# New lengths in the layout's own clock, twelve more attention units on VectorE, and a new table of urgencies

## The chip, the cores and the metric

One core of one Trainium2 chip runs the whole program. The metric is the device time of one execution in microseconds. "Before" is the median of three executions; one further execution was recorded by the hardware profiler, and all instruction durations below come from that one.

## The reference

Two kinds of layer alternate twice over one sequence of 2048 rows of 512 numbers: attention with 32 heads of 16 and a single shared key and value head, then a gated mixer.

```python
def _A_ref(x, wq, wk, wv, wo):            # H = 32, Dh = 16
    q = (x @ wq).reshape(B, S, H, Dh) ...  # one k and one v for all heads
    scores = einsum('bhqd,bkd->bhqk', q, k) * Dh ** (-0.5)
    p = softmax(scores, axis=-1)
    o = einsum('bhqk,bkd->bhqd', p, v)
    return o.reshape(B, S, H * Dh) @ wo

def _B_ref(x, w_in, w_sp, b_sp, w_out):    # F = 1792, Fh = 896
    z = gelu(einsum('bsd,df->bsf', x, w_in))
    z1, z2 = z[..., :Fh], layernorm(z[..., Fh:])
    g = einsum('ts,bsf->btf', w_sp, z2) + b_sp
    return einsum('bsf,fd->bsd', z1 * g, w_out)

x = x + A(layernorm(x)); x = x + B(layernorm(x))   # and both once more
```

The scores are 32 x 2048 x 2048 numbers in each of the two attention layers, and every one of them needs an exponential.

## The kernel before

**Units and blocks.** Attention is cut into 32 groups for each layer. A group is one set of query rows and heads whose output is 128x512, and it meets 16 key tiles. One group against one key tile is a *unit*: 512 queries and heads in each of four row strips, so four *blocks* of 128x512 scores. A score block is a matmul of 32 contracted rows (L990), and up to four of them, in different row strips of TensorE, run side by side.

**Two ways to the exponential.** Most units go to ScalarE: `push_slot` puts three or two blocks into one of two fixed groups of PSUM banks (banks 0 to 2, banks 3 and 4, in turn), and one ScalarE instruction (L1016) turns them into `P_ring`, a ring of 20 blocks. Then one step of four matmuls (L1035), side by side in four column strips, adds the unit to the group's sum in bank 6. The other units go to VectorE (`block_dve`): each block gets a side bank (5 or 7), and VectorE turns it into 16-bit integers whose bits are read as bf16, an approximate power of two (L1134). When the unit's four blocks are there, three additions inside SBUF (L1147, L1149, L1151) make four shifted copies, and five steps of four matmuls (L1167) add the five, each with its own weight, to the group's sum. A VectorE unit so takes five steps on TensorE where a ScalarE unit takes one. The tiles of these units live in a ring of six in `big`, of which one unit uses five.

How many of a group's 16 key tiles go to VectorE is a digit of `ON_DVE`, one string for each layer, for groups 4 to 31. The first groups have fixed shares of their own (`ATT`).

**Everything else runs between the blocks.** While attention runs, the finished row tiles go on: the output projection (`wo_tiles`), layernorm (`ln_tiles`), the mixer's first product (`b_front`, L690 with `w_in_r`), and parts of the big product with `w_sp` (`mix_stage`, L690 with `z2n`), whose partial sums VectorE adds (L1498) and which go to DRAM and come back. After the last group of layer 1 only the rest of the mixer is left (`mix_late`, L684).

**Who sets the order.** Nothing is ordered at run time. `_Graph.schedule` walks through all operations with a clock of its own, engine by engine, from lengths written into the code (`dur`, and `lat` until a reader may start), and at each free engine picks the ready operation with the smallest priority. `URGENCY` adds a number between -3 and 3 to the priority of named parts (`unit.1.63 pe` is the matmuls of VectorE units of layer 1 when 63 groups have been opened). The chosen order is emitted as one fixed stream for each engine with semaphore waits; the chip then runs these streams. Lengths in the code therefore never change a duration on the chip, they change the order, and with it who waits for whom. TensorE charges `SWITCH` for a change of tiling (full array, 32-row strips, 32-column strips). If TensorE has been busy for less than 55% of the last 3.4 us on this clock, `filler` puts in matmuls with no effect on the result (L716 on a free bank, L724 adding zeros).

The lines that the diff touches in the old kernel:

```python
def dve(fn, us, r, w, prio=5):
    return op("dve", fn, us, r=r, w=w, prio=prio)
...
main["last"] = op("act", act_e, 0.065 + n * 0.4267, r=[tk], ...)
...
us += SWITCH if o.mode != last_mode else 0.0
...
ON_DVE = [[0] * 4 + [int(c) for c in s] for s in (
    "4344343435423243434344233232",
    "4344433444333433434433244221")]
```

Of the kernel before, what the change touches and what calls it, by code (L numbers as in the profile page):

```python
# [38 lines left out]
SWITCH = 0.105  # L39
PE_LAT = 0.20  # L40
SEM_LAT = 0.06
# [4 lines left out]
URGENCY = {  # L46
# [26 lines left out]
}  # L73
# [10 lines left out]
AHEAD_US = 1.0  # L84
AHEAD_EPS = 0.05
PAIRS = False
PAIR_AHEAD = 0.12
# [57 lines left out]
class _Graph:  # L145
# [70 lines left out]
    def schedule(self):  # L216
# [15 lines left out]
        free = {e: True for e in ENGS}  # L232
        last_mode = 0
        open_rows = frozenset()
        bank_free = [True] * 8
# [12 lines left out]
        def push(t, what, x):  # L248
            nonlocal cnt
            cnt += 1  # L250
            heapq.heappush(ev, (t, cnt, what, x))
# [145 lines left out]
        while True:  # L397
            moved = True
            while moved:
                moved = False  # L400
                for e in ENGS:
                    if free[e]:
# [18 lines left out]
                        if e == "pe":  # L421
                            us += SWITCH if o.mode != last_mode else 0.0
                            past.append((now + us, o.work))
                            last_mode = o.mode
                            if o.opens is not None:
                                pv_open = o.opens
                            if beside(o):
                                us = BESIDE
                                open_rows = open_rows | o.rows
                            else:  # L430
                                open_rows = o.rows
                        push(now + us, 0, e)
                        for x in (o,) if o.mate is None else (o, o.mate):
# [118 lines left out]
def bass_interleave_layers__grouped_kv_mqa__mixer_gmlp__prompt_kernel(  # L552
# [127 lines left out]
    def dve(fn, us, r, w, prio=5):  # L680
        return op("dve", fn, us, r=r, w=w, prio=prio)

# [187 lines left out]
    def ln_tiles(t0, n, xT, keys, per_tile, prio=5, by_dma=False):  # L870
# [3 lines left out]
        for t in ts:  # L874
            i = t % CT
            dve(lambda e, i=i, t=t: e.bn_stats(st1[:, i, :], X[:, t, :]), 0.66, [("X", t)], [("st1", i)], prio)  # L876
            if not by_pool:
                dve(lambda e, i=i: e.bn_aggr(mv1[:, i, :], st1[:, i:i + 1, :]), 0.18, [("st1", i)], [("mv1", i)], prio)
# [114 lines left out]
    def push_slot(n):  # L993
# [21 lines left out]
        def act_e(e):  # L1015
            return e.activation(P_ring[:, s0:s0 + n, :], bank32(b0, n).rearrange("p (k q) -> p k q", k=n), ACTF.Exp,  # L1016
                                scale=E_SCALE)
        main["last"] = op("act", act_e, 0.065 + n * 0.4267, r=[tk], w=[("P", s0 + k) for k in range(n)], prio=3)
        for k, (u, j) in enumerate(blocks):
# [95 lines left out]
    def block_dve(x, j, slot_op):  # L1115
# [14 lines left out]
        if slot_op is not None:  # L1130
# [4 lines left out]
            ph16[:, tiles[0], j * QC:(j + 1) * QC], bank32(tk.bank), PH_BIAS, 0.0, op0=ALU.add, op1=ALU.max),  # L1135
            0.66, [tk], BIG(tiles[0]) if k == 0 else [("phj", tiles[0], k)], P_R)
        if PAIRS:
# [5 lines left out]
        if k == 3:  # L1143
            spread["todo"].pop(0)
            base = BIG(tiles[0]) + [("phj", tiles[0], i) for i in range(1, 4)]
            r0, r2, r4 = tiles[0], tiles[2], tiles[4]
            dve(lambda e: e.tensor_scalar(ph16[:, r2, :], ph16[:, r0, :], float(PH_A[2]), None, op0=ALU.add), 0.63, base,  # L1147
                BIG(r2), P_PH)
            dve(lambda e: e.tensor_scalar(two_rows(tiles[1], tiles[3]), two_rows(r0, r2), float(PH_A[1]), None,  # L1149
                                          op0=ALU.add), 1.16, base + BIG(r2), BIG(tiles[1]) + BIG(tiles[3]), P_PH)  # L1150
            dve(lambda e: e.tensor_scalar(ph16[:, r4, :], ph16[:, r0, :], float(PH_A[4]), None, op0=ALU.add), 0.63, base,  # L1151
                BIG(r4), P_PH)
# [23 lines left out]
    def finish_group(gi):  # L1176
# [20 lines left out]
        if RECP and t0 < DT_O:  # L1197
            op("pool", lambda e: e.tensor_tensor(rden[:, par, :, :], src()[:, :, :, DH],  # L1198
                                                 mone[:, 0:1, None].to_broadcast([P, CT, 4]), ALU.pow),
               0.4 + 0.19 * 16, r=[tk, "mone"], w=[("rden", par)], prio=pr)  # L1200
        else:
# [354 lines left out]
    def sums_lead(n, chain):  # L1556
# [61 lines left out]
    ON_DVE = [[0] * 4 + [int(c) for c in s] for s in (  # L1618
        "4344343435423243434344233232",
        "4344433444333433434433244221")]  # L1620

# [62 lines left out]
```

## Time and profile before

| what | value |
|---|---|
| median of three executions | 1662.25 us (1659.72 to 1663.79) |
| the profiled execution, its own time | 1657.53 us |
| its span in the profile | 1655.7 us |
| granted TensorE clock | 0.999 |
| TensorE matmul busy | 1574.8 us (95%) |
| ScalarE busy | 1557.9 us (94%) |
| VectorE busy | 1454.4 us (88%) |
| GpSimd busy | 371.5 us (22%) |
| 1313 exponentials, L1016 | 1487.3 us busy |

Busy time is the union of an engine's instruction records. On VectorE and ScalarE a record outlasts the moment at which the next instruction starts, so a full engine is better counted by the steps from start to start. The busy time of TensorE also holds the fillers and the waiting inside a pipelined matmul.

### The profile page before, as it was taken

The numbers are of one execution on the slowest core, as the hardware profiler recorded it, in microseconds if no ns is written. First come the engines' busy times: TensorE is split into PE (matmuls) and PEld (weight loads), VectorE is DVE, ScalarE is ACT, GpSimd is POOL, SyncE is SP. The second block draws the span as 40 slices with busy tenths as digits, with TensorE's granted clock in tenths as the row PEclk, the third lists the DMA queues.
The fourth block names the chain that finished last, engine by engine and source line by source line (L and its number), as shares of the span: only waits on it lengthen the run. The fifth ranks groups of instructions, "written<-read, shape, count | busy, mean of one in ns | idle before, by whom it ended". The sixth has DMA issues, their size and how long they took to land.

```text
span 1655.7 us, 45720 instructions
## 1 busy us (share of the span) xinstructions
PE 1574.8 (95%) x20407; PEld 529.0 (32%) x20421; DVE 1454.4 (88%) x2248; ACT 1557.9 (94%) x1362; POOL 371.5 (22%) x481
## 2 busy tenths in 40 slices
PE   8899999999999999999999999999899999989999
PEld 3222223232332232334533222233233323323344
DVE  8999989998899898877869999899989999798677
ACT  7999999999999999999299999999999999999970
POOL 3131221213221114000531321211422112220012
PEclk9999999999999999999999999999999999999999
DMA  8000010101321240555511000100033102305665
GB/s 199 17 18 8 9 26 5 21 8 40 84 56 40 62 93 5 132 150 148 157 48 24 17 8 14 21 12 16 12 87 88 38 22 77 54 30 151 173 162 151
DMA packets 173270, 102.75 MB, mean 62 GB/s; under 512 B 135056, under 2 KB 145680, under 8 KB 173072
## 3 DMA queue, kind: packets, MB, share of 16 engines
q1 hardware_dynamic: 173072, 99.81, 23.9%
q8 instruction: 160, 2.62, 0.7%
q14 instruction: 38, 0.31, 0.1%
HBM read 36.34 MB, written 31.46 MB: 41 GB/s over the span
## 4 chain that ended last, share of the span: by engine, by line
ACT 78%; PE 19%; DVE 2%; issue 0%; DMA 0%; SPq 0%; POOL 0%; DVEq 0%
ACT P_ring L1016 76%; PE ps_all L690 7%; PE ps_all L990 4%; PE ps_all L684 4%; PE ps_all L1167 2%; PE ps_all L1035 2%; ACT z2n L1398 1%; DVE big L1134 0%; DMA X<-in_A_x_dram 0%; DVE st L1441 0%; ACT L1016 0%; ACT L1398 0%; PE ps_all L898 0%; PE ps_all L724 0%; PE ps_all L1573 0%
## 5 line engine op out<-in xcount | busy, mean ns | idle before, releaser
L1016 ACT ACTIVATE P_ring<-ps_all 128x1024 bf16<-128x1024 f32 (+1 forms) x1313 | 1487.3, 1352 | 13.1 <-PE ps_all L990 12.0
L990 PE MATMUL ps_all<-qT,kT_rep 32*128 32x512 bf16 x4096 | 593.0, 385 | 67.2 <-ACT P_ring L1016 59.2
L1134 DVE TENSOR_SCALAR big<-ps_all 128x512 int16<-128x512 f32 x816 | 540.2, 685 | 86.0 <-PE ps_all L990 78.8
L1198 POOL TENSOR_TENSOR rden<-o_rows,small 128x16 f32<-128x16 bf16 x56 | 177.6, 3172 | 742.6 <-DMA o_rows<-oT 742.6
L990 PEld LDWEIGHTS ps_all<-qT,kT_rep 32*128 32x128 bf16 x4096 | 148.9, 91 | 601.5 <-ACT P_ring L1016 507.5
L1167 PE MATMUL ps_all<-big,V_ph 128*32 128x512 bf16 x4080 | 337.7, 383 | 2.1 <-DVE big L1149 0.7
L1035 PE MATMUL ps_all<-P_ring,V_ph 128*32 128x512 bf16 x3280 | 310.7, 386 | 1.3 <-DVE oT L1238 0.6
L1149 DVE TENSOR_SCALAR big<-big 128x4096 int16<-128x4096 int16 x204 | 249.1, 1221 | 0.5
L1147 DVE TENSOR_SCALAR big<-big 128x2048 int16<-128x2048 int16 x204 | 140.6, 689 | 3.3 <-PE ps_all L1167 0.8
L1151 DVE TENSOR_SCALAR big<-big 128x2048 int16<-128x2048 int16 x204 | 138.9, 693 | 2.5 <-PE ps_all L1167 2.2
L1167 PEld LDWEIGHTS ps_all<-big,V_ph 128*32 128x32 bf16 x4080 | 92.8, 95 | 128.9 <-issue 60.7
L1035 PEld LDWEIGHTS ps_all<-P_ring,V_ph 128*32 128x32 bf16 x3280 | 81.1, 94 | 142.6 <-issue 116.9
L724 PE MATMUL ps_all<-ones,zeros 128*32 128x512 bf16 x1200 | 101.3, 386 | 0.0
L690 PE MATMUL ps_all<-xnTA,z2n 128*32 128x512 bf16 x1344 | 94.3, 381 | 0.1
L820 POOL TENSOR_TENSOR small<-st 128x4 f32<-128x4 f32 (+5 forms) x50 | 18.8, 392 | 325.4 <-DVE st L876 267.2
L1270 DVE TENSOR_TENSOR X<-ps_all,X 128x512 bf16<-128x512 f32 x64 | 43.9, 686 | 25.5 <-PE ps_all L690 15.7
L690 PE MATMUL ps_all<-w_in_r,xo 128*32 128x448 bf16 x960 | 60.5, 355 | 0.3 <-DVE big L1134 0.2
L1212 POOL TENSOR_TENSOR o_norm<-o_rows,rden 128x128 bf16<-128x128 bf16 x112 | 57.4, 533 | 4.3
L690 PE MATMUL ps_all<-xo,w_in_r 128*32 128x512 bf16 (+2 forms) x1120 | 55.7, 327 | 0.3 <-DVE z1c L1388 0.3
L1498 DVE TENSOR_TENSOR big<-ps_all,big 128x512 f32<-128x512 f32 x56 | 38.3, 686 | 19.2 <-PE ps_all L690 18.9
L1363 DVE CAST z2n<-ps_all 128x448 bf16<-128x448 f32 x60 | 37.2, 620 | 18.5 <-PE ps_all L690 18.1
L1547 POOL TENSOR_TENSOR z1c<-big,z1c 128x512 bf16<-128x512 f32 (+1 forms) x47 | 45.1, 979 | 34.1 <-DVE big L1542 33.7
(113 smaller groups left out, 1081.7 us busy)
## 6 DMA issues: line engine op xcount, KB each, us to landing
gp_scratch<-big SPq DMA_DIRECT2D x112, 256.0 KB, 2.2
big<-gp_scratch SPq DMA_DIRECT2D x98, 256.0 KB, 3.0
big<-gp_scratch SPq DMA_DIRECT2D x28, 128.0 KB, 2.8
out_dram<-X SPq DMA_DIRECT2D x16, 128.0 KB, 2.4
w_in_r<-in_B_w_in_dram SPq DMA_DIRECT2D x1, 1792.0 KB, 8.3
X<-in_A_x_dram SPq DMA_DIRECT2D x3, 512.0 KB, 6.6
bsp<-in_B_b_sp_dram SPq DMA_DIRECT2D x8, 128.0 KB, 3.9
w_out_r<-in_B_w_out_dram SPq DMA_DIRECT2D x1, 896.0 KB, 5.5
```

The source lines that it names most:

```text
L684: return e.matmul(out, w, mv, start=start, stop=stop)
L690: ins = e.matmul(out[32 * j:32 * j + 32, :], w[:, 32 * j:32 * j + 32], mv, tile_position=(0, 32 * j), start=start, stop=stop)
L724: ins = e.matmul(bank32(PVB)[32 * j:32 * j + 32, :], zeros[:, 0:32], mv, tile_position=(0, 32 * j), start=False, stop=False)
L990: return e.matmul(out, kT_rep[32 * j:32 * j + 32, a, u[1] * P:(u[1] + 1) * P], qT[32 * j:32 * j + 32, q, :], tile_position=(32 * j, 0), st ...
L1016: return e.activation(P_ring[:, s0:s0 + n, :], bank32(b0, n).rearrange("p (k q) -> p k q", k=n), ACTF.Exp, scale=E_SCALE)
L1035: ins = e.matmul(bank32(PVB)[32 * j:32 * j + 32, :], V_ph[:, NPH, kt, :], P_ring[:, s, :], tile_position=(0, 32 * j), start=first, stop=last)
L1134: o = dve(lambda e: e.tensor_scalar(ph16[:, tiles[0], j * QC:(j + 1) * QC], bank32(tk.bank), PH_BIAS, 0.0, op0=ALU.add, op1=ALU.max), 0.66 ...
L1147: dve(lambda e: e.tensor_scalar(ph16[:, r2, :], ph16[:, r0, :], float(PH_A[2]), None, op0=ALU.add), 0.63, base, BIG(r2), P_PH)
L1149: dve(lambda e: e.tensor_scalar(two_rows(tiles[1], tiles[3]), two_rows(r0, r2), float(PH_A[1]), None, op0=ALU.add), 1.16, base + BIG(r2), ...
L1151: dve(lambda e: e.tensor_scalar(ph16[:, r4, :], ph16[:, r0, :], float(PH_A[4]), None, op0=ALU.add), 0.63, base, BIG(r4), P_PH)
L1167: ins = e.matmul(bank32(PVB)[32 * j:32 * j + 32, :], V_ph[:, a, kt, :], big[:, tiles[a], j * QC:(j + 1) * QC], tile_position=(0, 32 * j), ...
L1198: op("pool", lambda e: e.tensor_tensor(rden[:, par, :, :], src()[:, :, :, DH], mone[:, 0:1, None].to_broadcast([P, CT, 4]), ALU.pow), 0.4 ...
```

## The change

The `dve` helper now plans an instruction 85 ns shorter and lets its reader start 75 ns after that; several VectorE lengths are raised by some 25 or 60 ns ahead of this; the exponential is planned 12 ns shorter with 230 ns until its reader; the change of tiling is charged only as far as TensorE was not idle just before; TensorE's own delay to a reader goes from 0.20 to 0.15 us; one GpSimd length is lowered. Twelve units net go from ScalarE to VectorE: five in layer 0 (groups 8, 11, 16, 17, 22 and 23 get one more, group 27 one less) and seven in layer 1 (groups 5, 8, 14, 23 and 24 one more, group 26 two more). The table of urgencies is replaced. `SWIDLE` is defined and not used.

```diff
-PE_LAT = 0.20
+PE_LAT = 0.15
 URGENCY = {
-    "/b_front.0.0.4 pe": 1.5, "/b_front.0.0.4/ln_tiles.0.0.4": -3, "/b_front.0.12.3 pe": 0.5,
...
+    "/b_front.0.0.4 pe": 0.5, "/b_front.0.0.4/ln_tiles.0.0.4": -1.5, "/b_front.0.12.3 pe": -1,
...
+SWIDLE = 1.0
...
+        pe_end = 0.0
...
-                            us += SWITCH if o.mode != last_mode else 0.0
+                            us += max(0.0, SWITCH - (now - pe_end)) if o.mode != last_mode else 0.0
...
+                            pe_end = now + us
...
     def dve(fn, us, r, w, prio=5):
-        return op("dve", fn, us, r=r, w=w, prio=prio)
+        return op("dve", fn, max(0.06, us - 0.085), r=r, w=w, prio=prio, lat=0.075)
...
-        main["last"] = op("act", act_e, 0.065 + n * 0.4267, r=[tk], w=[("P", s0 + k) for k in range(n)], prio=3)
+        main["last"] = op("act", act_e, 0.053 + n * 0.4267, r=[tk], w=[("P", s0 + k) for k in range(n)], prio=3, lat=0.23)
...
             ph16[:, tiles[0], j * QC:(j + 1) * QC], bank32(tk.bank), PH_BIAS, 0.0, op0=ALU.add, op1=ALU.max),
-            0.66, [tk], BIG(tiles[0]) if k == 0 else [("phj", tiles[0], k)], P_R)
+            0.685, [tk], BIG(tiles[0]) if k == 0 else [("phj", tiles[0], k)], P_R)
...
-               0.4 + 0.19 * 16, r=[tk, "mone"], w=[("rden", par)], prio=pr)
+               2.98, r=[tk, "mone"], w=[("rden", par)], prio=pr, lat=0.17)
...
     ON_DVE = [[0] * 4 + [int(c) for c in s] for s in (
-        "4344343435423243434344233232",
-        "4344433444333433434433244221")]
+        "4344443535424343435444223232",
+        "4444533444433433434543444221")]
```

More of the change, by code (lines that the diff above doesn't have):

```diff
@@ L875, in ln_tiles @@
             i = t % CT
-            dve(lambda e, i=i, t=t: e.bn_stats(st1[:, i, :], X[:, t, :]), 0.66, [("X", t)], [("st1", i)], prio)
+            dve(lambda e, i=i, t=t: e.bn_stats(st1[:, i, :], X[:, t, :]), 0.685, [("X", t)], [("st1", i)], prio)
             if not by_pool:
@@ L1146, in block_dve @@
             r0, r2, r4 = tiles[0], tiles[2], tiles[4]
-            dve(lambda e: e.tensor_scalar(ph16[:, r2, :], ph16[:, r0, :], float(PH_A[2]), None, op0=ALU.add), 0.63, base,
+            dve(lambda e: e.tensor_scalar(ph16[:, r2, :], ph16[:, r0, :], float(PH_A[2]), None, op0=ALU.add), 0.69, base,
                 BIG(r2), P_PH)
             dve(lambda e: e.tensor_scalar(two_rows(tiles[1], tiles[3]), two_rows(r0, r2), float(PH_A[1]), None,
-                                          op0=ALU.add), 1.16, base + BIG(r2), BIG(tiles[1]) + BIG(tiles[3]), P_PH)
-            dve(lambda e: e.tensor_scalar(ph16[:, r4, :], ph16[:, r0, :], float(PH_A[4]), None, op0=ALU.add), 0.63, base,
+                                          op0=ALU.add), 1.22, base + BIG(r2), BIG(tiles[1]) + BIG(tiles[3]), P_PH)
+            dve(lambda e: e.tensor_scalar(ph16[:, r4, :], ph16[:, r0, :], float(PH_A[4]), None, op0=ALU.add), 0.69, base,
                 BIG(r4), P_PH)
```

56 rows, old and new, of the table URGENCY are left out of this document.

## The prediction

> **What bounds the kernel now.** I read the page's busy shares and its chain of waits first, then the groups kept apart by shape.
>
> ```profile
> span 1655.7 us, 45720 instructions
> ...
> PE 1574.8 (95%) x20407; PEld 529.0 (32%) x20421; DVE 1454.4 (88%) x2248; ACT 1557.9 (94%) x1362; POOL 371.5 (22%) x481
> ...
> ACT 78%; PE 19%; DVE 2%; issue 0%; DMA 0%; SPq 0%; POOL 0%; DVEq 0%
> ```
>
> ```profile
> L1016 ACT ACTIVATE P_ring<-ps_all 128x1536 bf16<-128x1536 f32 x655 | 1023.1, 1562 | 2.7 <-PE ps_all L990 1.7
> L1016 ACT ACTIVATE P_ring<-ps_all 128x1024 bf16<-128x1024 f32 x657 | 750.9, 1143 | 10.4 <-PE ps_all L990 10.3
> ...
> L1134 DVE TENSOR_SCALAR big<-ps_all 128x512 int16<-128x512 f32 x816 | 540.2, 685 | 86.0 <-PE ps_all L990 78.8
> ...
> L1149 DVE TENSOR_SCALAR big<-big 128x4096 int16<-128x4096 int16 x204 | 249.1, 1221 | 0.5
> ```
>
> Three engines look nearly full, but the chain of waits lies on ScalarE for 78% of the span, and its exponentials were kept waiting 13.1 us (2.7 and 10.4). VectorE's idle time stands ahead of L1134, where it waits for scores. The windows of busy time by stage, and VectorE's timeline:
>
> ```profile
> 898.20:1040.60 142.40, 134.08 (x1602) 39.70 (x1597) 135.42 (x196) 142.36 (x127) 34.17 (x24) 1.00 0.06 13
> 1040.60:1186.10 145.50, 135.29 (x1835) 44.10 (x1834) 134.44 (x205) 145.12 (x125) 35.76 (x48) 1.00 0.07 14
> ...
> 1513.50:1588.20 74.70, 74.11 (x1025) 24.22 (x1025) 46.59 (x76) 74.66 (x68) 1.92 (x7) 1.00 0.65 174
> 1588.20:1655.70 67.50, 63.32 (x464) 29.53 (x462) 55.62 (x99) 17.04 (x14) 17.79 (x16) 1.00 0.52 148
> ```
>
> ```profile
> 410.15 0.68 DVE L1270 TENSOR_TENSOR X<-ps_all,X 128x512 bf16<-128x512 f32 x1
> 410.74 0.68 DVE L1134 TENSOR_SCALAR big<-ps_all 128x512 int16<-128x512 f32 x1
> 411.34 0.68 DVE L1240 CAST oT<-ps_all 128x512 bf16<-128x512 f32 x1
> ```
>
> After span, the columns are TensorE, its weight loads, VectorE, ScalarE and GpSimd. The first two rows are groups 1 to 14 of layer 1: ScalarE is full (142.36 of 142.40). Just after the last group (fourth row) it has little to do, and TensorE is busy 63.32 of 67.50. The timeline shows why 685 ns is not what a VectorE instruction costs: the next starts 0.60 us later, 85 ns before the record ends. Counted so, by records less 85 ns, VectorE's work is 1386 us, 84% of the span. Exponentials likewise start 1.330 us apart behind one of three blocks and 0.903 behind one of two (medians of the starts), not 1.562 and 1.143. Counted so, ScalarE lost 20.6 us between exponentials (8.7 and 9.3 of it in the two layers' dense stretches, 77 to 671 us and 898 to 1513 us). It is the bound; VectorE has room.
>
> **ScalarE.** The changed kernel's order holds 646 exponentials of three blocks and 647 of two, where there were 655, 657 and one of a single block: 9 x 1.330 + 10 x 0.903 + 0.48 (0.903 less the 0.427 of one block) = 21.5 us less, nearly all on the path. One unit is 21.5 / 12 = 1.79 us.
>
> A rule of the Trainium skill (ScalarE: Activation LUTs, What ACT_TABLE_LOAD costs) prices an ACTIVATE at 186 ns plus 0.833 ns an element, with back-to-back ones overlapping by 93 ns; as an estimate from that page a step would be 1.372 or 0.946 us and the saving 22.3 us. The measured starts decide.
>
> **VectorE.** Twelve units add 48 of L1134 at 0.60 and twelve each of L1147, L1149 and L1151 at 0.60, 1.13 and 0.60 (records less 85 ns): 4.73 us a unit, 56.8 in all, 1386 to 1443 us. Over the whole span that fits. By stage it does not everywhere. I summed these costs over each stretch between the evacuations of groups (L1238, L1240), in the old order and the new, and set against them the length that ScalarE alone would allow (the measured one less 1.79 us for each unit taken away):
>
> | groups | before, VectorE of length | after, VectorE of ScalarE's length |
> |---|---|---|
> | layer 0, 4 to 14 | 221.3 of 248.0 (89%) | 231.0 of 244.4 (95%) |
> | layer 0, 15 to 26 | 248.3 of 290.5 (85%) | 261.0 of 283.4 (92%) |
> | layer 1, 1 to 14 | 259.9 of 287.9 (90%) | 275.3 of 282.5 (97%) |
> | layer 1, 15 to 23 | 179.7 of 202.7 (89%) | 186.2 of 200.9 (93%) |
> | layer 1, 24 to 28 | 105.6 of 124.7 (85%) | 113.8 of 119.3 (95%) |
>
> What counts is the share that VectorE can hold. The best that the trace shows is 95.1% over 60 us (from 64 us on) and 93.5% over 120 us, both while ScalarE set the pace, so neither is a ceiling; 100% would be one. At a share s each row takes the larger of its two times, and the excess over ScalarE's length sums to 0 at 98%, 4.3 at 96% (275.3 / 0.96 = 286.8), 7.8 at 95%, 13.5 at 94%, 20.5 at 93% and 24 at 92.5%. I take 95.5%, 6 us: just over the nearest row, since a VectorE that is late has its next work waiting.
>
> **TensorE.** A step of four side by side takes 0.217 us and a change of tiling 0.105:
>
> ```profile
> 402.19 0.39 PE L990 MATMUL ps_all<-qT,kT_rep 32*128 32x512 bf16 x3
> 402.51 0.62 PE L690 MATMUL ps_all<-z2n 128*32 128x512 bf16 x8
> 403.06 0.39 PE L990 MATMUL ps_all<-qT,kT_rep 32*128 32x512 bf16 x2
> ```
>
> Three scores and a change take 0.32 us, two steps and a change 0.55. The twelve units add 60 steps of L1167 and remove 12 of L1035, +10.4 us; fillers go from 325 to 307, -3.9. With the changes of tiling the orders sum to 1493 and 1501 us. In the attention stretches that is +2.6 us in layer 0 and -2.3 in layer 1, hidden behind ScalarE: TensorE between one exponential's scores and the next averages 1.064 us before and 1.076 after, against exponentials of 1.09.
>
> **The tail is not hidden.** Behind the last L1035 the new order puts 24 more steps of the mixer's second stage (5.2 us), 8 of `w_in` columns of 448 (1.5), 4 of width 384 (0.65) and two fillers less (-0.4); with changes of tiling 64.1 us become 70.6. TensorE's idle time there is 4.2 us (67.50 less 63.32), so the cost is between 2.3 and some 8 us, the upper end if the last tile's chain (output projection, layernorm, normalization), now queued behind 11 us of other matmuls, opens new gaps. I take 6: the old gaps are waits of that chain and stay. Between the layers TensorE, last on the path there, gets 41.1 to 42.7 us: +1, between 0 and 2. The other lengths only reorder: new GpSimd and delay constants change no count, and the DMA queue gets the same transfers; I price them at nothing, covered by ScalarE's backlog, or at the first rival's excess where that is gone.
>
> **Sum.** -21.5 + 6 + 1 + 6 = -8.5, say -9 us. The profiled execution took 1657.5 us (span 1655.7 and 1.8 around it) and would become 1648.5. The median, 1662.25, lies 4.7 above that execution; on it the forecast is 1653.
>
> **Rivals.**
> *VectorE becomes the bound (slower).* Place: groups 1 to 14 of layer 1, at 97% even without a stall, then groups 4 to 14 of layer 0. Mechanism: L1134 needs a score block in one of two side banks, the matmuls of a unit wait on TensorE's fixed queue for the additions, and the scores for ScalarE stand behind them. For it: the 78.8 us that L1134 waited for scores, so some idle time may be inherent. Against: much of that wait was pacing by ScalarE. At 92.5% the excess is 24 us and the sum +10: 1672. It decides at 94%, where the excess eats the 14.5.
> *The new order also removes stalls.* The new lengths match the measured steps (0.60; 1.333 and 0.906 against 1.330 and 0.903), the old ones were too long on VectorE by 0.06. If VectorE holds 97% or more (1 us) and 5 of the 20.6 lost us go: -18.5, 1644.
> *TensorE takes part.* Pairs of intervals in which TensorE's work exceeds the exponentials' rise from 375 to 444, their excess from 115 to 122 us. If all 7 reach the path: -1.5, 1661.
> *VectorE's additions collide with GpSimd.* The power at L1198 runs 178 us, 11% of the span. Were an addition that meets one held for half its 3.17 us, the 36 new ones would lose 36 x 0.11 x 1.6 = 6 us: -2.5, 1660. The trace speaks against it: L1149 waited 0.5 us in all over 204 and is no longer beside L1198 (1218 ns) than away from it (1221).
> The Trainium skill (SBUF — State Buffer, Who interferes with whom) states that rule: VectorE in a two-port mode and GpSimd share a port pair, and whichever comes second blocks fully. By it this rival would stand; the rows show VectorE not held.
> That the move does not happen is excluded by the count of exponentials.
>
> **How the numbers follow.** A measurement tells 0.3%, 5 us, from no change. Forecast 0.50 (0.44 of it beyond 5 us, 0.06 within), VectorE-bound 0.20, fewer stalls 0.13, TensorE 0.14 (0.03 faster, 0.09 same, 0.02 slower), port 0.03 (0.02 same, 0.01 slower). Faster 0.60, same 0.17, slower 0.23. The forecast's own range is 1646 to 1658 (share 94.5 to 98%, tail 2.3 to 8). For 8 in 10 it reaches into both neighbours: 1642 to 1668.
>
> **What would show it.** Right: 1293 exponentials, some 1466 us busy; idle time ahead of L1016 up from 13 to 15 to 25 us, mostly in layer 1's first 14 groups; VectorE near 95% there by steps; last exponential ending near 1573 us instead of 1587.5, and some 74 us behind it. Wrong: those 14 groups longer than 287.9 us (first rival), less idle time ahead of L1016 (second), or 68 us behind the last exponential, as before (the tail's 6).

## The result and the profile after

| | before | after |
|---|---|---|
| median of six executions | 1662.47 us (1658.42 to 1663.79) | 1653.18 us (1650.59 to 1654.32) |
| profiled execution, its own time | 1657.53 us | 1654.32 us |
| its span | 1655.7 us | 1652.5 us |

The ratio is 0.9945, with a 95% interval of 0.9931 to 0.9959: 9.3 us less, outside the 0.3% that a measurement tells from no change.

Not all of the 9.3 us belongs to the change. In many executions TensorE's granted clock falls to half for a few microseconds, at places that differ from run to run. Executions with a mean clock of 1.000 took 1656.1 to 1656.9 us before (measured beside the experiments) and 1650.59 and 1650.63 us after, so some 6 us are the change's; the rest is that the runs of before behind the median held more of these dips. Below, "undisturbed" means the length of a stage in a run that had no dip there; such lengths repeat to 0.1 to 0.4 us.

The page of the changed kernel, the lines that answer to those of before:

```profile
span 1652.5 us, 45935 instructions
...
PE 1590.0 (96%) x20490; PEld 538.2 (33%) x20490; DVE 1487.8 (90%) x2332; ACT 1544.7 (93%) x1342; POOL 372.3 (23%) x481
...
ACT 48%; PE 38%; DVE 12%; issue 1%; DMA 1%; POOL 0%; DVEq 0%; SPq 0%
...
L1025 ACT ACTIVATE P_ring<-ps_all 128x1024 bf16<-128x1024 f32 (+1 forms) x1293 | 1474.2, 1305 | 23.3 <-PE ps_all L999 19.9
```

The chain of waits, 78% on ScalarE before, is now 48% ScalarE, 38% TensorE and 12% VectorE. The exponentials (L1025, before L1016) are 20 fewer and waited 23.3 us for scores and buffers where they had waited 13.1. VectorE's groups (L1143 and L1158, before L1134 and L1149):

```profile
L1143 DVE TENSOR_SCALAR big<-ps_all 128x512 int16<-128x512 f32 x864 | 563.0, 681 | 44.8 <-PE ps_all L999 42.5
L1158 DVE TENSOR_SCALAR big<-big 128x4096 int16<-128x4096 int16 x216 | 263.2, 1218 | 0.7 <-PE ps_all L1176 0.2
```

VectorE now waits 44.8 us ahead of its score blocks, not 86.0: it took in 48 blocks more and nearly halved its idle time there. The additions still start without a wait (0.7 us over 216) and last as long as before (1218 against 1221 ns).

By stage, as in the prediction's table (a stage ends where a group's sum is taken out of bank 6). "Fewer exponentials" is 1.08 us, the 21.5 / 20 of the forecast, for each exponential that the stage lost or got; the last column is what the difference holds beyond that.

| stage | before | after | difference | forecast | exponentials | rest |
|---|---|---|---|---|---|---|
| layer 0, to group 3 | 112.6 | 107.7 | -4.9 | 0 | -3.2 | -1.7 |
| layer 0, 4 to 14 | 248.0 | 246.2 | -1.8 | -3.6 | 0 | -1.8 |
| layer 0, 15 to 26 | 290.5 | 287.2 | -3.3 | -7.2 | -8.6 | +5.3 |
| layer 0, 27 to 31 | 122.3 | 127.7 | +5.4 | +1.8 | +3.2 | +2.2 |
| between the layers | 124.8 | 119.6 | -5.2 | +1 | -2.2 | -3.0 |
| layer 1, 1 to 14 | 287.9 | 286.7 | -1.2 | +0.4 | -1.1 | -0.1 |
| layer 1, 15 to 23 | 202.7 | 205.4 | +2.7 | -1.8 | -1.1 | +3.8 |
| layer 1, 24 to 28 | 124.7 | 116.6 | -8.1 | -5.4 | -8.6 | +0.5 |
| layer 1, 29 to 31 | 74.7 | 77.4 | +2.7 | 0 | 0 | +2.7 |
| tail | 67.5 | 74.3 | +6.8 | +6 | 0 | +6.8 |

The columns add to -6.9 measured and -8.8 forecast, with -21.6 for the exponentials. (The first row of before holds a dip of 3.4 us at 32.7 us, worth some 1.0: v1 below, the same kernel up to layer 1, took 111.6 without it. The row of groups 24 to 28 and the tail are from undisturbed runs, since the profile of after has a dip at 1474.5 us.)

Part of two rows is not waiting. One of ScalarE's activations of the mixer, which with the loads of its tables around it takes 7.3 us, ran across the border at 360.6 us before, and behind that of 353.9 us after:

```profile
359.76 4.68 ACT L1398 ACTIVATE z2n<-z2n 128x5376 bf16<-128x5376 bf16 x1
```

```profile
377.25 4.68 ACT L1407 ACTIVATE z2n<-z2n 128x5376 bf16<-128x5376 bf16 x1
```

So some 2 us of ScalarE's own work left groups 4 to 14 of layer 0 for groups 15 to 26: of the rests -1.8 and +5.3, that leaves about 0 and +3.3.

In the windows, after the span, the columns are TensorE, its weight loads, VectorE, ScalarE and GpSimd. First before, four of the stages:

```profile
360.60:651.10 290.50, 276.43 (x3722) 88.86 (x3711) 259.68 (x392) 290.14 (x251) 68.10 (x91) 1.00 0.21 54
651.10:773.40 122.30, 120.88 (x1687) 40.22 (x1690) 96.76 (x152) 122.27 (x107) 13.47 (x17) 1.00 0.48 126
898.20:1186.10 287.90, 269.37 (x3436) 83.80 (x3431) 269.86 (x401) 287.48 (x251) 69.93 (x72) 1.00 0.07 14
1186.10:1388.80 202.70, 197.34 (x2655) 63.20 (x2655) 187.17 (x277) 202.57 (x180) 45.12 (x43) 1.00 0.21 57
```

Then after, the same four and the last two:

```profile
353.90:641.00 287.10, 279.26 (x3810) 91.96 (x3813) 267.38 (x409) 286.05 (x245) 67.47 (x74) 1.00 0.20 48
641.00:768.70 127.70, 124.83 (x1747) 41.98 (x1743) 97.41 (x159) 126.04 (x110) 15.48 (x32) 1.00 0.55 147
888.30:1175.10 286.80, 275.54 (x3443) 86.63 (x3439) 280.51 (x424) 286.22 (x250) 73.52 (x71) 1.00 0.08 14
1175.10:1380.50 205.40, 202.50 (x2747) 67.07 (x2747) 191.73 (x287) 203.66 (x179) 44.28 (x44) 1.00 0.23 62
...
1499.90:1577.20 77.30, 76.45 (x1057) 24.91 (x1053) 47.68 (x77) 76.51 (x67) 1.92 (x7) 1.00 0.68 171
1577.20:1652.50 75.30, 70.95 (x612) 33.26 (x604) 59.88 (x106) 16.70 (x14) 17.64 (x16) 1.00 0.60 181
```

Before, ScalarE is full in all four (290.14 of 290.50 and so on). After, ScalarE has 1.1 to 1.7 us of idle time in three of the four, and TensorE closes up: 279.26 of 287.10 where it was 276.43 of 290.50, 202.50 of 205.40 where it was 197.34 of 202.70. In groups 29 to 31 of layer 1 (from 1499.90) it is busy 76.45 of 77.30, and in the tail (from 1577.20) 70.95 of 75.30 where it was 63.32 of 67.50. In groups 1 to 14 of layer 1 ScalarE stays full (286.22 of 286.80) beside a VectorE at 280.51. Busy time by records hides ScalarE's short waits, since a record outlasts the start of the next by some 0.23 us (1.562 less 1.330). Counted from each start to the next exponential's, less 1.330 or 0.903, ScalarE lost 4.3, 1.7, 4.3 and 3.3 us in these four stages before and 6.7, 4.8, 5.0 and 6.9 after. The chain of waits cut to groups 15 to 26 of layer 0, before and after:

```profile
by line: ACT P_ring L1016 85.3%; PE ps_all L690 5.4%; PE ps_all L990 3.3%; ACT z2n L1398 3.2%; PE ps_all L1035 1.1%; ACT L1016 0.9%; PE ps_all L1167 0.8%; ACT L1398 0.4%; DVE z2n L1363 0.2%; issue 0.1%
```

```profile
by line: ACT P_ring L1025 29.8%; PE ps_all L999 17.0%; PE ps_all L699 14.0%; PE ps_all L1176 8.9%; PE ps_all L1044 8.0%; DVE big L1143 6.4%; ACT z2n L1407 3.3%; DVE big L1158 2.4%; DVE big L1160 2.1%; PE ps_all L733 1.6%; DVE big L1156 1.6%
```

ScalarE's exponentials go from 85.3% of the chain to 29.8%. What replaces them is a bit of each: scores and mixer products on TensorE (17.0 and 14.0), both kinds of attention sum (8.9 and 8.0), VectorE's units (6.4, 2.4, 2.1 and 1.6). This is not one engine in place of another.

### The profile page after: what moved, and what is told of

The parts are those of the page before. It is cut to its first block, busy times and chain, and to the rows that moved or that the text cites. A ratio compares the mean times of both kernels' runs of the same rounds, so it can differ in the third digit from the quotient of the medians.

```text
span 1652.5 us, 45935 instructions
## 1 busy us (share of the span) xinstructions
PE 1590.0 (96%) x20490; PEld 538.2 (33%) x20490; DVE 1487.8 (90%) x2332; ACT 1544.7 (93%) x1342; POOL 372.3 (23%) x481
## 4 chain that ended last, share of the span: by engine, by line
ACT 48%; PE 38%; DVE 12%; issue 1%; DMA 1%; POOL 0%; DVEq 0%; SPq 0%
ACT P_ring L1025 47%; PE ps_all L699 13%; PE ps_all L999 11%; PE ps_all L1176 5%; PE ps_all L1044 5%; DVE big L1143 4%; PE ps_all L693 3%; DVE big L1158 2%; ACT z2n L1407 1%; DVE big L1160 1%; DVE big L1156 1%; PE ps_all L733 1%; DVE z1c L1397 0%; PE ps_all L907 0%; DVE st L1450 0%
## 5 line engine op out<-in xcount | busy, mean ns | idle before, releaser
L1025 ACT ACTIVATE P_ring<-ps_all 128x1024 bf16<-128x1024 f32 (+1 forms) x1293 | 1474.2, 1305 | 23.3 <-PE ps_all L999 19.9
L999 PE MATMUL ps_all<-qT,kT_rep 32*128 32x512 bf16 x4096 | 599.6, 385 | 42.4 <-ACT P_ring L1025 31.2
L1143 DVE TENSOR_SCALAR big<-ps_all 128x512 int16<-128x512 f32 x864 | 563.0, 681 | 44.8 <-PE ps_all L999 42.5
L1176 PE MATMUL ps_all<-big,V_ph 128*32 128x512 bf16 x4320 | 359.3, 384 | 8.6 <-DVE big L1158 5.8
L1207 POOL TENSOR_TENSOR rden<-o_rows,small 128x16 f32<-128x16 bf16 x56 | 180.8, 3228 | 759.5 <-DMA o_rows<-oT 759.5
L1044 PE MATMUL ps_all<-P_ring,V_ph 128*32 128x512 bf16 x3232 | 302.8, 386 | 2.5 <-DVE oT L1249 1.3
L1158 DVE TENSOR_SCALAR big<-big 128x4096 int16<-128x4096 int16 x216 | 263.2, 1218 | 0.7 <-PE ps_all L1176 0.2
L1156 DVE TENSOR_SCALAR big<-big 128x2048 int16<-128x2048 int16 x216 | 148.9, 689 | 7.2 <-PE ps_all L1176 4.8
L1160 DVE TENSOR_SCALAR big<-big 128x2048 int16<-128x2048 int16 x216 | 146.5, 686 | 0.2 <-PE ps_all L1176 0.2
L733 PE MATMUL ps_all<-ones,zeros 128*32 128x512 bf16 x1060 | 91.3, 384 | 0.0
L1507 DVE TENSOR_TENSOR big<-ps_all,big 128x512 f32<-128x512 f32 x56 | 38.4, 685 | 38.8 <-PE ps_all L699 37.2
L1221 POOL TENSOR_TENSOR o_norm<-o_rows,rden 128x128 bf16<-128x128 bf16 x112 | 49.9, 466 | 4.2
L699 PE MATMUL ps_all<-z2n 128*32 128x512 bf16 x672 | 48.1, 382 | 0.2 <-DVE big L1143 0.2
```

The lines of the kernel that those rows point to most:

```text
L699: ins = e.matmul(out[32 * j:32 * j + 32, :], w[:, 32 * j:32 * j + 32], mv, tile_position=(0, 32 * j), start=start, stop=stop)
L733: ins = e.matmul(bank32(PVB)[32 * j:32 * j + 32, :], zeros[:, 0:32], mv, tile_position=(0, 32 * j), start=False, stop=False)
L999: return e.matmul(out, kT_rep[32 * j:32 * j + 32, a, u[1] * P:(u[1] + 1) * P], qT[32 * j:32 * j + 32, q, :], tile_position=(32 * j, 0), st ...
L1044: ins = e.matmul(bank32(PVB)[32 * j:32 * j + 32, :], V_ph[:, NPH, kt, :], P_ring[:, s, :], tile_position=(0, 32 * j), start=first, stop=last)
L1143: o = dve(lambda e: e.tensor_scalar(ph16[:, tiles[0], j * QC:(j + 1) * QC], bank32(tk.bank), PH_BIAS, 0.0, op0=ALU.add, op1=ALU.max), 0.68 ...
L1176: ins = e.matmul(bank32(PVB)[32 * j:32 * j + 32, :], V_ph[:, a, kt, :], big[:, tiles[a], j * QC:(j + 1) * QC], tile_position=(0, 32 * j), ...
```

## The experiments

**What each part is worth.** Four kernels: the new lengths alone (e1), the new units alone (e2), the whole change with the old table (e3), and with the old units (e4).

```diff
-        "4344443535424343435444223232",
-        "4444533444433433434543444221")]
+        "4344343435423243434344233232",
+        "4344433444333433434433244221")]
```

That is e4 against after; e2 is the same two lines the other way, against before. In e3 the old `URGENCY` stands in the changed kernel, and in e1 both the old table and the old units.

> New lengths alone: the old shares of units and the old table, with all the changed lengths. My theory (the gain is the 21.5 us of exponentials moved off ScalarE, which VectorE takes only if the order keeps it near 96%; lengths and table serve that and bring nothing alone): 1313 exponentials stay, and a table chosen for other lengths orders worse, so 1660 to 1690 us, not faster than before. Rival A (the order alone brings the gain): about 1653. Rival B (the units alone bring it): about 1662, as before.

> Twelve more units alone: the new shares with the old lengths and the old table. My theory: the exponentials fall to 1293 and ScalarE's steps by 21.5 us, but the layout takes VectorE to be 10% slower than it is and the table is for other units, so ScalarE waits more: 1655 to 1680, no gain. Rival A (order alone): 1662 or more. Rival B (units alone): 1641 to 1653.

> New lengths and new units, with the old table of urgencies. My theory: the exponentials are the new 1293, but the old table's choices for TensorE delay scores and sums, which shows as idle time ahead of the exponentials: 1658 to 1685. Rival (the table is a detail, lengths and units carry the gain): 1650 to 1656.

> New lengths and new table with the old shares of units. My theory: 1313 exponentials, ScalarE's 21.5 us come back, VectorE falls to some 90% in the first 14 groups of layer 1, and the table, chosen for the other units, adds pauses: 1664 to 1690. Rival A (the order alone brings the gain): 1650 to 1656.

| kernel | median, us | ratio to before | interval |
|---|---|---|---|
| e1, lengths alone | 1692.58 | 1.0206 | 1.0188 to 1.0223 |
| e2, units alone | 1744.00 | 1.0518 | 1.0500 to 1.0536 |
| e3, all but the table | 1698.63 | 1.0252 | 1.0231 to 1.0273 |
| e4, all but the units | 1703.06 | 1.0267 | 1.0245 to 1.0289 |

All four lie above what was expected of them, by 3 to 64 us. Every one of these parts and pairs makes the kernel 2 to 5% slower; the table alone, and table and units without the lengths, were not tried. It looks as if a table of urgencies fits only the lengths and units that it was made for. e3 against after says that the new table is worth some 45 us on this set of lengths and units; e4 against e1 says that on the old units it costs 10. So a part's worth depends on the others, and the 6 us can't be shared out among the three. What a misfit looks like, from e2's exponentials kept apart by shape:

```profile
L1016 ACT ACTIVATE P_ring<-ps_all 128x1536 bf16<-128x1536 f32 x646 | 998.8, 1546 | 45.9 <-PE ps_all L990 45.2
L1016 ACT ACTIVATE P_ring<-ps_all 128x1024 bf16<-128x1024 f32 x647 | 727.2, 1124 | 77.5 <-PE ps_all L990 77.3
```

They waited 123.4 us (45.9 and 77.5) for scores, where those of before waited 13.1. The units are those of after; what differs is the order and, with it, the number of fillers.

**What sets the pace, before and after.** The next kernels keep the order of every stream and put extra work on one engine in one stage. If that engine sets the pace there, the stage grows by the whole load; if it has room, by nothing. For VectorE, the first and last of each unit's three additions are cut in four pieces; this is the edit of v1 (before) and v2 (after), for groups 4 to 14 of layer 1:

```diff
+            cuts = 4 if now["layer"] == 1 and 60 <= x["no"] <= 70 else 1
+            def in_parts(row, add):
+                def run(e):
+                    for c in range(cuts):
+                        q = slice(2048 * c // cuts, 2048 * (c + 1) // cuts)
+                        ins = e.tensor_scalar(ph16[:, row, q], ph16[:, r0, q], add, None, op0=ALU.add)
+                    return ins
+                return run
...
-            dve(lambda e: e.tensor_scalar(ph16[:, r4, :], ph16[:, r0, :], float(PH_A[4]), None, op0=ALU.add), 0.63, base,
+            dve(in_parts(r4, float(PH_A[4])), 0.63, base,
...
```

> The kernel before, same order, with more VectorE work in groups 4 to 14 of layer 1: the first and the last of a unit's three additions are cut into four pieces each, 240 more instructions at an estimated 0.067 us (0.60 us a step for 2048 columns, of which 0.53 is the columns) = 16 us. My theory (VectorE has about 10% to spare there before the change): the 28 us that it idles in groups 1 to 14 take most of it, +0 to +5 us. Rival (VectorE's idle time there is inherent waiting for scores, so that it is full already): +12 to +16.

> The changed kernel, same order, with the same cuts, 258 more VectorE instructions, 17 us by the same estimate. My theory (VectorE at 96% is what limits these groups after the change): +13 to +18 us. Rival (ScalarE or TensorE still limits them): +0 to +5.

The size of the load, from the additions in groups 1 to 14 of layer 1 in after and then in v2, kept apart by shape:

```profile
L1156 DVE TENSOR_SCALAR big<-big 128x2048 int16<-128x2048 int16 x49 | 33.9, 692 | 0.5
L1160 DVE TENSOR_SCALAR big<-big 128x2048 int16<-128x2048 int16 x49 | 33.5, 691 | 0.0
```

```profile
L1162 DVE TENSOR_SCALAR big<-big 128x512 int16<-128x512 int16 x344 | 74.9, 287 | 0.4
...
L1162 DVE TENSOR_SCALAR big<-big 128x2048 int16<-128x2048 int16 x12 | 8.5, 732 | 0.1
```

By records less 85 ns, 344 pieces at 0.202 and 12 whole ones at 0.647 us take 77.3 us where 98 took 59.4: 17.9 us more. In v1 the same count gives 17.3. The stage in v1 and in v2:

```profile
897.20:1188.70 291.50, 272.76 (x3436) 84.13 (x3431) 283.96 (x641) 288.71 (x251) 71.10 (x72) 1.00 0.07 13
```

```profile
888.70:1190.80 302.10, 280.30 (x3446) 85.73 (x3442) 297.42 (x681) 290.84 (x250) 73.55 (x71) 1.00 0.08 13
```

v1's VectorE is busy 283.96 us, beside a ScalarE at 288.71 of 291.50. Before, 17.3 us more on VectorE made the stage 3.6 us longer (287.9 to 291.5), 21% of the load. After, 17.9 made it 15.4 longer (286.7 to 302.1), 86%. The medians are 1661.08 us (ratio 1.0018, 1.0004 to 1.0032) and 1666.70 (1.0052, 1.0033 to 1.0071). VectorE had room before and has next to none now, as the chain of waits of v2 in that stage says:

```profile
by line: DVE big L1143 36.4%; DVE big L1162 24.5%; DVE big L1167 16.5%; PE ps_all L699 2.9%; PE ps_all L999 2.9%; DVE st L1459 2.1%; PE ps_all L1185 2.0%; DVE oT L1258 1.8%; DVE z1c L1406 1.5%; issue 1.4%; PE ps_all L1044 1.4%; DVE z2n L138
```

VectorE's unit instructions alone (L1143, and L1162 and L1167, which are L1156, L1160 and L1158 of after) hold 77.4% of it.

**Is it VectorE instead of ScalarE there?** s2 loads ScalarE and q2 TensorE, in the same groups of the changed kernel. In s2 106 exponentials of three blocks become 318 of one: three at 0.48 less one of 1.330, 0.11 us for each of the 106, some 11 us in all. In q2 61 steps that add zeros, 13.2 us at 0.217, go ahead of attention sums.

```diff
+        if now["layer"] == 1 and 61 <= main["open"] <= 71 and n == 3:
+            def act_e(e):
+                for k in range(n):
+                    ins = e.activation(P_ring[:, s0 + k, :], bank32(b0 + k), ACTF.Exp, scale=E_SCALE)
+                return ins
```

```diff
+        if now["layer"] == 1 and 61 <= main["open"] <= 71 and not first and not last and kt % 2:
+            one = pe_pv
+            def pe_pv(e):
+                add_zeros(e, 2)
+                return one(e)
...
```

> The changed kernel, same order, with more ScalarE work in groups 4 to 14 of layer 1: 106 exponentials of three blocks are given as three of one block, 212 more instructions at an estimated 0.05 us (1.330 less 3 x 0.427) = 11 us. My theory (VectorE limits, ScalarE is 4 us behind it: 282.5 of 286.8): +5 to +8 us. Rival one (ScalarE alone limits): +11. Rival two (ScalarE has slack there): +0 to +3.

> The changed kernel, same order, with more TensorE work in groups 4 to 14 of layer 1: 61 more steps of four matmuls that add zeros, 13.2 us at 0.217. My theory (TensorE waits there for VectorE and ScalarE): +0 to +6 us. Rival (TensorE's fixed queue limits these groups): +10 to +13.

```profile
890.00:1188.50 298.50, 278.17 (x3443) 85.83 (x3439) 283.54 (x423) 298.40 (x462) 72.21 (x71) 1.00 0.07 13
```

s2's stage is 298.5 us, 11.8 longer: ScalarE's load comes through whole, though VectorE's did too. So the idea that VectorE had taken the pace over was wrong; the two are tied, and a load on either is paid. q2's stage is 292.2 us, 5.5 longer, 42% of its load: TensorE has some room there. The medians are 1663.47 (1.0027, 1.0016 to 1.0039) and 1656.31 (0.9986, 0.9975 to 0.9998).

**The later groups.** x1 puts the zeros of q2 into groups 15 to 26 of layer 0 (70 steps, 15.2 us) and 15 to 23 (57, 12.4) and 29 to 31 (19, 4.1) of layer 1. x2 cuts VectorE's additions in four in the first two of these.

```diff
+        gr = main["open"] - (13, 61)[now["layer"]] + 4
+        if (15 <= gr <= 26 if not now["layer"] else 15 <= gr <= 23 or gr >= 29) and not first and not last and kt % 2:
...
```

```diff
+            gr = x["no"] - (12, 60)[now["layer"]] + 4
+            cuts = 4 if 15 <= gr <= (23 if now["layer"] else 26) else 1
...
```

> The changed kernel, same order, with more TensorE work where VectorE is not full: 146 steps of four matmuls that add zeros, 0.217 us each, 31.7 us in all, in groups 15 to 26 of layer 0 and in groups 15 to 23 and 29 to 31 of layer 1, one at every second unit of ScalarE. My theory (in these groups TensorE, busy for 97 to 99% of them, took part of the relief): at least 70% of the price, +22 to +32 us. Rival (TensorE is as it was in groups 4 to 14 of layer 1, where 13.2 us cost 5.5): +10 to +15.

> The changed kernel, same order, with more VectorE work in groups 15 to 26 of layer 0 and 15 to 23 of layer 1: the cut additions there, 444 more instructions at the 0.069 us that the same cut cost in the earlier groups, 31 us. My theory (VectorE, at 91% by steps, has room there): +0 to +8 us. Rival (VectorE limits here too, as in groups 1 to 14 of layer 1, where 17.9 us cost 15.4): +24 to +30.

The stage of groups 15 to 23 of layer 1, in x1 and then in x2:

```profile
1184.10:1398.10 214.00, 211.83 (x2976) 71.27 (x2975) 194.14 (x288) 207.15 (x180) 43.68 (x44) 1.00 0.21 60
```

```profile
1189.60:1405.70 216.10, 208.69 (x2750) 67.00 (x2750) 204.15 (x480) 207.10 (x179) 47.14 (x44) 1.00 0.23 60
```

x1's stages grew from 287.2 to 296.2 (60% of the load), from 205.4 to 214.0 (69%) and from 77.4 to 81.0 us (88%), 21.3 us in all, just under what was expected; 1674.73 us, ratio 1.0099 (1.0080 to 1.0118). The chain of waits of x1 in groups 15 to 23:

```profile
by line: PE ps_all L999 25.7%; PE ps_all L699 24.5%; PE ps_all L1183 15.8%; PE ps_all L1044 11.0%; PE ps_all L733 8.3%; ACT P_ring L1025 6.2%; DVE big L1150 5.2%; DVE big L1165 1.1%; DVE big L1163 0.9%; DVE big L1167 0.8%; issue 0.5%; DVE o
```

TensorE's scores (25.7), mixer products (24.5), attention sums (15.8 and 11.0) and zeros (8.3) hold 85% of it and ScalarE 6.2%; without the zeros ScalarE held 47.5% there, and before the change 80.1%.

x2's load is 18.9 and 14.3 us by records less 85 ns, and its stages grew by 14.2 (287.2 to 301.4) and 10.7 (205.4 to 216.1), 75% of each; 1677.30 us, ratio 1.0107 (1.0092 to 1.0122). That is 24.9 us where 0 to 8 were expected, and the rival named 24 to 30: VectorE had some 9% of its time free in those groups by records less 85 ns (261 of 287.2 us and 186 of 205.4), and this was not room. The likely way, which no run takes apart, is that with the order fixed a late addition holds TensorE's next step, and that step the scores for ScalarE: counted by starts as above, ScalarE lost 21.2 and 17.0 us there, not 6.7 and 6.9.

**The same loads before the change.** m1 is the kernel before with s2's load in groups 4 to 14 of layer 1, x2's in 15 to 23 there, and x1's in groups 15 to 26 of layer 0 and 29 to 31 of layer 1.

```diff
+        if now["layer"] == 1 and 61 <= main["open"] <= 71 and n == 3:
...
+        if (gr >= 29 if now["layer"] else 15 <= gr <= 26) and not first and not last and kt % 2:
...
+            cuts = 4 if now["layer"] and 71 <= x["no"] <= 79 else 1
...
```

> The kernel before, same order, with one kind of extra work in each of four places, to be read stage by stage against its own profile: ScalarE in groups 4 to 14 of layer 1 (108 exponentials of three blocks given as three of one, some 11.8 us), VectorE in groups 15 to 23 of layer 1 (the cut additions of 31 units, some 13 us), TensorE in groups 15 to 26 of layer 0 (some 15 us of steps that add zeros) and in groups 29 to 31 of layer 1 (some 4 us). My theory (before the change ScalarE alone sets the pace, and the layer's last groups are TensorE's): ScalarE's at full price, +11 to +13; VectorE's +1 to +5, where the changed kernel paid 10.7; TensorE's +2 to +6 in layer 0, where it paid 9.1, and +3 to +4 in the last groups. Rival (each engine's lateness was passed on before just as after): VectorE's +9 to +11 and TensorE's +8 to +10.

Its stages of layer 1 with ScalarE's and with VectorE's load:

```profile
907.70:1208.50 300.80, 272.85 (x3436) 83.67 (x3431) 272.14 (x406) 300.63 (x467) 68.36 (x72) 1.00 0.07 13
1208.50:1414.60 206.10, 200.09 (x2657) 63.97 (x2657) 197.01 (x458) 204.50 (x181) 44.77 (x43) 1.00 0.21 57
```

They were 287.9 and 202.7 us without: 12.9 and 3.4 more, as expected, and ScalarE is full in the first (300.63 of 300.80). TensorE's load in layer 0 cost 7.1 us, over the 2 to 6 that were expected and under the rival's 8 to 10. The median is 1683.83 us (1.0163, 1.0149 to 1.0176). How much of a load came through, by stage and engine:

| groups, engine | before | after |
|---|---|---|
| layer 1, 4 to 14, ScalarE | 12.9 of some 11.8 us | 11.8 of some 11 |
| layer 1, 4 to 14, VectorE | 3.6 of 17.3 (21%) | 15.4 of 17.9 (86%) |
| layer 1, 4 to 14, TensorE | not tried | 5.5 of 13.2 (42%) |
| layer 1, 15 to 23, VectorE | 3.4 of 12.2 (28%) | 10.7 of 14.3 (75%) |
| layer 1, 15 to 23, TensorE | not tried | 8.6 of 12.4 (69%) |
| layer 0, 15 to 26, TensorE | 7.1 of 15.4 (46%) | 9.1 of 15.2 (60%) |
| layer 1, 29 to 31, TensorE | 3.1 of 4.1 (75%) | 3.6 of 4.1 (88%) |

Before, ScalarE set the pace, and other engines' loads came through by a fifth to a half except in the last groups. After, they come through by 42 to 88%, VectorE's by 75% and more, while ScalarE's still do so whole.

**The tail.** t1 is the changed kernel without two urgencies that push the last tile's output projection back:

```diff
-    "/turn_tile.1.15": 2,
...
-    "/wo_tiles.1.15.1 pe": 3,
```

> The changed kernel with two entries of the table left out, both of the last row tile, so that its output projection is no longer queued behind 11 us of other matmuls; the order is the same up to the last group's transposes. My theory (the longer tail is the moved matmuls themselves, with TensorE busy through it): the tail stays within 2 us, 1649 to 1653 as the changed kernel. Rival (the queue ahead of the last tile's chain is what costs): 3 to 6 us less.

Its tail took 74.7 us against 74.3, and its runs at clock 1.000 took 1651.01 to 1652.00 us against 1650.6: letting that chain go first brings nothing. The median is 1653.10 (0.9976, 0.9965 to 0.9987). TensorE behind the last exponential, before and after:

```profile
1587.50:1655.70 68.20, 64.02 (x480) 29.95 (x478) 55.86 (x100) 17.73 (x14) 17.79 (x16) 1.00 0.52 149
```

```profile
1576.20:1652.50 76.30, 71.95 (x632) 33.78 (x624) 60.51 (x107) 17.68 (x15) 17.64 (x16) 1.00 0.61 182
```

TensorE was idle 4.18 us (68.20 less 64.02) and is idle 4.35 (76.30 less 71.95). The whole growth is busy time, the matmuls that the order moved there. Some 1 us of this profile's tail is a wait of VectorE for a transfer (1.55 us ahead of L1507 at 1582.59 us), which v2's tail of 74.3 us doesn't have: there TensorE is idle 3.56 us.

## Why the prediction was right, and where it was not

**The total.** Forecast 1653.0, measured 1653.18 us. Two errors cancel in it. The working gave -8.5 to -9 us against before's profiled execution, and stage by stage -6.9 came out. The other 2 us came in with the step to the median, for which the prediction carried before's 4.7 us over: before's median (now 1662.47) lies 4.9 us above its profiled execution, after's 2.6 above its undisturbed one, and -6.9 - 4.9 + 2.6 is -9.2. How many dips the six executions held was luck.

**ScalarE: the saving right, the waiting too low.** 1293 exponentials, 21.6 us by the stages against 21.5. They were busy 1474.2 us, not 1466; the waiting ahead of them, 23.3 us, is within the 15 to 25 named, but that is by records. By starts, the count that the prediction itself prefers, ScalarE lost 23.9 us before (20.6 by the prediction), and 40.7 in t1, whose order up to the tail is that of after and which has no dip: 17 more, where the sum had 6 for it. It is not where it was looked for either: groups 1 to 14 of layer 1 hold 0.7 of the 17, the stages from group 15 to 31 some 11, and the stretch between the layers, where TensorE is last on the path, 5.

**VectorE, 6 us: wrong in place and kind.** The step took a share of 95.5% as what VectorE can hold, and charged nearly all of the 6 to groups 1 to 14 of layer 1. The length there was nearly met (286.7 against 288.3, 96%), but not by ScalarE waiting. The stage lost one exponential, not three units' worth, as some of the blocks of neighbouring groups run in it. And the share isn't a limit: in groups 24 to 28 of layer 1 VectorE's steps fill 113.9 of 116.6 us, 98%, and that stage gained 2.7 us more than forecast. The first rival, 24 us at 92.5%, is excluded by the same row; v2 and s2 show that it was near, since VectorE has no room left there.

**TensorE "hidden behind ScalarE": the step that failed.** It was priced at nothing, by averages over the attention stretches: 1.076 us against exponentials of 1.09. By place, four of the five stages from group 15 on (rest column: 5.3, 2.2, 3.8 and 2.7; groups 24 to 28 of layer 1 only 0.5) gave back 14.0 us, 12 without the activation that moved, more than the 7 of the rival that had TensorE take part. The chain in them turned from ScalarE to TensorE's lines, and x1 and m1 show that a load on TensorE comes through there by 60 to 88%, before by 46 and 75%. The 12 us can't be shared between TensorE and VectorE: in x2 VectorE's loads came through by 75% in two of these stages. What the runs show is that these groups had little room beside ScalarE, and the counts say which work was added there; no run takes that work alone away. In two of the four it is not the added units. Groups 27 to 31 of layer 0 have one unit less on VectorE, and 60 matmuls more (1687 to 1747), 44 of them fillers; groups 29 to 31 of layer 1 have no unit more, and the mixer's second product moved in. The prediction found this move only in the tail:

```profile
L690 PE MATMUL ps_all<-xnTA,z2n 128*32 128x512 bf16 x380 | 27.7, 382 | 0.1
```

```profile
L699 PE MATMUL ps_all<-xnTA,z2n 128*32 128x512 bf16 x456 | 32.5, 382 | 0.3 <-DVE big L1507 0.3
```

These are groups 29 to 31 before and after. Groups 24 to 28 fell from 200 of them to 32, and by the starts of the matmuls 72 went to groups 29 to 31 and 96, the 24 steps of the forecast, to the tail. An average over a stretch can't show that.

**A stall that went, where +1 was forecast.** Between the layers the stage gained 3.0 us beyond its exponentials: the second copy of the transposed rows for layer 1 (L800, now L809) waited 4.36 us for TensorE before, at 805.32 us, and waits 1.20 after, at 798.19. Groups 4 to 14 of layer 0 gained nothing but the activation that left them, and the first groups some 0.7 once the dip's 1.0 is taken off. The rival of fewer stalls expected 5 us less waiting of ScalarE, and by starts that waiting grew; its stall went in a place where ScalarE isn't full. No run tells which of the three parts brought it.

**The tail, right.** +6.8 against 6, in [2.3, 8], "the old gaps stay" shown by the two windows and by t1. Some 76 us lie behind the last exponential in the profile, which ends at 1576.2 us; 74 and 1573 were forecast. The dip accounts for 2.7 of the latter, the wait for a transfer for 1 of the former.

**The port, rightly dismissed.** With twelve units more the additions were held no longer than before: 1218 against 1221 ns, 0.7 us of idle time over 216. The Trainium skill's rule (SBUF — State Buffer, Who interferes with whom), by which whichever of the two comes second blocks fully, isn't seen on VectorE in these rows; GpSimd's power (L1207), at 3228 ns against 3172, is the one that grew.

In sum: -21.6, some +12 for the late groups where 6 had been put on VectorE, +6.8 for the tail, some -4.5 in groups 0 to 14 of layer 0 and between the layers, where +1 had stood (1.0 of it before's dip), and +0.4 in groups 1 to 14 and 24 to 28 of layer 1: -6.9. The late groups cost 6 us more than was charged to VectorE, and these early places gave 5.5 more than forecast. That the sum was met rests on these two being alike, which is luck.

## What to carry to other kernels

Price a shift of work between engines stage by stage and against the engine that comes next in each stage, not by averages: here 21.6 us came off the bound engine and some 12 were given back in groups where the other two had little room. Look also at what else moved with it: two of these stages got none of the shifted units, but other work of TensorE. Where the order of each engine is fixed, a share of free time says little of how much load an engine can take (VectorE, 9% free, passed on 75% of 18.9 us); adding a harmless load to one engine in one stage, with the order kept, measures it in one run. Here a table of priorities went with one set of lengths and units, and undoing a part of such a change priced the misfit, not the part.

## What the runs showed of the hardware

TensorE's granted clock falls to half in the middle of this kernel, which keeps TensorE busy for 95 to 96% of the span; its profiles hold such dips of 3.4, 6.8 and 10.2 us. Windows of the profile of after, the dip between its neighbours; the clock is the third column from the end:

```profile
1470.00:1474.50 4.50, 3.50 (x39) 1.08 (x40) 4.43 (x9) 4.50 (x5) 2.40 (x11) 1.00 0.00 0
1474.50:1481.30 6.80, 6.80 (x50) 1.27 (x53) 4.92 (x8) 4.91 (x5) 0.12 (x1) 0.50 0.10 19
1481.30:1486.00 4.70, 4.70 (x72) 1.51 (x68) 4.32 (x8) 4.48 (x4) 2.67 (x3) 1.00 0.02 3
```

The 6.8 us at half clock made groups 24 to 28 of layer 1 119.3 us long, against 116.6 in the runs without it; in x2 a dip of the same length fell into these groups and made them 119.0. TensorE had been busy 3.50 of 4.50 us before it and was busy all of it in the dip. Dips fall in different places in different runs, and with a kernel as tight as this one they move a run's time by up to 7 us (before: 1656.1 at a mean clock of 1.000, 1663.2 at 0.994), as much as the change.

VectorE was kept 98% full over 117 us: in groups 24 to 28 of layer 1 its records, less the 85 ns of each that lie beside the next, fill 113.9 of 116.6 us (v2, whose order there is that of after).
